# P times V of a pooled attention: four float32r products on the whole array become float32 products on parts of it

## Chip, core and metric

The kernel runs on one core of a Trainium2 chip. The metric is the device time of one execution in microseconds; the median of three runs of the kernel before is 544.26 us (543.83 to 544.35).

## What is computed

Attention over keys and values that are averaged in groups of eight tokens, and behind it a gated MLP that mixes tokens. Eight batches, eight heads, 576 tokens, head size 64; 72 pooled tokens.

```
k_p = k.reshape(B, H, 72, 8, D).mean(axis=3)
v_p = v.reshape(B, H, 72, 8, D).mean(axis=3)
scores = scale * np.matmul(q, k_p.transpose(0, 1, 3, 2))
attn = exp(scores - max); attn = attn / (sum(attn) + 1e-09)
x = np.matmul(attn, v_p)             # heads side by side: (8, 576, 512)
h = np.maximum(x @ w_in, 0.0)        # 512 -> 1024
u, v = h[..., :512], h[..., 512:]
v_n = (v - mean(v)) / np.sqrt(var(v) + 1e-06)
v_s = np.einsum('ts,bsd->btd', w_spatial, v_n) + b_spatial[None, :, None]
out = (u * v_s) @ w_out
```

All inputs are float64 or float32 in memory; the output is float32.

## The kernel before

The work is cut into steps, and each step is a generator that records its instructions up to the next `yield`. The string `ORDER` names the steps one after the other; each name there advances its step by one piece. Nothing else sorts the instructions: what stands in a queue of an engine (TensorE = PE, VectorE = DVE, ScalarE = ACT, GpSimd = POOL, and SyncE = SP, which issues all DMAs) stands there in the order of `ORDER`, and an engine that waits holds up all that is behind it in its queue.

A name starts with the batch. `K`, `KT`, `V`, `W` load and pool keys and values; `Q` loads queries; `S` computes scores of a pair of heads g (four pairs) and their softmax; `T` and `Y` turn the probabilities so that the pooled tokens lie on the partitions (`Y` for the last 64 of the 576 tokens); `A` multiplies by V. Behind them come the MLP's steps `v` (second half of h, normalised), `u` (first half), `s` (mixing of tokens, then the gate) and `o` (output). Names with `w` load weights, which come as float64 and are put together as two float32r parts, high and low, on DVE, ACT and POOL.

Large products are made of float32r products: high by high, low by high, high by low. A product whose operands are plain float32 is one call in the program and two records on PE in the trace.

A pair of heads has 2 x 72 = 144 rows of probabilities per token. 128 of them are turned into the tile `pt_h`/`pt_l` (high and low part, lines 660 and 663 for batches 2 to 7, line 194/196 for 0 and 1), the other 16, of two pairs together 32 rows, into `pt_r` and, high and low, `pt_rr` (661, 666; 689, 691). In batches 0 and 1 PE turns them (676, 680, 728, 729); in the others DVE turns blocks of 32 by 32 (698, 702) and two DMAs through DRAM finish it. On the side of V, step `W` splits the pooled values under a mask that says to which head a row belongs (`vm_h`, `vm_l`, `vr_s`, `vr`; lines 517 to 531). `att_av` (lines 767 to 770) then makes four float32r products for each pair of heads and each half of the tokens (256 and 320), in one PSUM bank of the ring `mm`, which has four; the result is split into `xT` high (ACT, line 194) and low (DVE, 196 and 775).

The scores (line 634) are float32 products of 64 rows by 64 columns of the array, four of which lie in the four quarters; they go into the ring `s` of PSUM, two buffers of two banks each.

## Time and profile before

| | |
|---|---|
| median of three runs | 544.26 us |
| span of the profiled execution, first to last instruction | 543.1 us |
| PE busy | 519.7 us (96%) |
| DVE, ACT, POOL busy | 344.5, 287.3, 285.8 us |
| first matmul starts, last one ends | 8.40 and 540.0 us |

The profiled execution's own time is its span of 543.1 us and what lies around it; the median of the runs is 1.2 us above the span. In the trace a matmul's record is longer than the step from it to the next one, because matmuls overlap; how fast PE works is read from the starts of its rows.

### The profile page before, as it was taken

What the parts mean: (1) busy time and instruction counts of PE and PEld (TensorE: products, weight loads), DVE (VectorE), ACT (ScalarE), POOL (GpSimd) and SP (SyncE); (2) the same over time, 40 slices, a digit from 0 to 9 for tenths busy, and PEclk for the clock granted to TensorE, in tenths of its full rate; (3) what the DMA queues carried; (4) which work ended last, traced back from release to release, by engine and by line L of the source; (5) the groups of instructions that cost most, each with busy time, mean ns of one, the idle gap of its engine ahead of it and who ended that gap; (6) DMA issues with size and microseconds to landing.
All of it is one profiled execution on the core that took longest, in us unless ns stands there. A gap on an engine that the chain in (4) does not pass through costs nothing.

```text
span 543.1 us, 11804 instructions
## 1 busy us (share of the span) xinstructions
PE 519.7 (96%) x4317; PEld 468.6 (86%) x4317; DVE 344.5 (63%) x787; ACT 287.3 (53%) x919; POOL 285.8 (53%) x380
## 2 busy tenths in 40 slices
PE   3669999999999999999999999999999999999997
PEld 3556898988998999999898898998998898998996
DVE  3998989999966865775755756657743645234110
ACT  2677887545845566575464465565552544134122
POOL 3536666775488747764575965155345325124141
PEclk9979999999999999999999999999999999999999
DMA  7987654456447664654357133450053113000102
GB/s 216 286 208 151 155 144 120 107 118 171 139 154 188 176 160 116 161 148 114 93 138 186 64 86 74 121 159 1 25 181 98 56 39 95 21 0 21 59 20 78
DMA packets 125674, 63.11 MB, mean 116 GB/s; under 512 B 84272, under 2 KB 109360, under 8 KB 125616
## 3 DMA queue, kind: packets, MB, share of 16 engines
q1 hardware_dynamic: 125616, 62.35, 43.0%
q8 instruction: 34, 0.56, 0.4%
q14 instruction: 24, 0.20, 0.1%
HBM read 44.92 MB, written 17.40 MB: 115 GB/s over the span
## 4 chain that ended last, share of the span: by engine, by line
PE 92%; DVE 3%; DMA 2%; ACT 1%; SPq 1%; issue 0%; ACTq 0%
PE mm L879 19%; PE mm L861 19%; PE mm L905 18%; PE mm L818 17%; PE s_ps L634 4%; PE mm L834 3%; DMA qt<-in_q 2%; PE tp L767 2%; PE tp L770 2%; PE tp L768 2%; PE mm L880 2%; PE tp L769 2%; PE mm L881 2%; PE tp L374 1%; DVE vr_s L517 1%
## 5 line engine op out<-in xcount | busy, mean ns | idle before, releaser
L861 PE MATMUL mm<-xT,win_h 128*128 128x256 f32 (+1 forms) x512 | 103.7, 296 | 0.0
L893 POOL TENSOR_TENSOR gT<-g,gT 128x256 fp32r<-128x256 f32 x64 | 47.4, 746 | 88.3 <-ACT gT L890 88.3
L861 PEld LDWEIGHTS mm<-xT,win_h 128*128 128x128 f32 x512 | 83.0, 188 | 1.7
L818 PE MATMUL mm<-win_h,xT 128*128 128x512 f32 x256 | 80.5, 395 | 0.0
L905 PE MATMUL mm<-wout_h,gT 128*128 128x512 f32 (+1 forms) x264 | 80.4, 387 | 0.0
L879 PE MATMUL mm<-wT_h,vn_h 128*128 128x320 f32 (+1 forms) x256 | 76.1, 297 | 0.1
L879 PE MATMUL mm<-wT_h,vn_l 128*128 128x320 f32 (+1 forms) x256 | 75.6, 295 | 0.0
L879 PE MATMUL mm<-wT_l,vn_h 128*128 128x320 f32 (+1 forms) x256 | 75.6, 295 | 0.0
L861 PE MATMUL mm<-xT,win_l 128*128 128x320 f32 (+1 forms) x256 | 75.5, 295 | 0.0
L884 DVE TENSOR_TENSOR g<-mm,ru 128x320 f32<-128x320 f32 (+1 forms) x64 | 28.6, 452 | 72.9 <-PE mm L881 62.1
L828 POOL TENSOR_TENSOR vn_l<-vv,vn_h 128x512 fp32r<-128x512 f32 x32 | 42.6, 1337 | 39.3 <-ACT vn_h L826 39.0
L617 POOL TENSOR_TENSOR e<-e,rs 128x576 f32<-128x576 f32 (+1 forms) x32 | 42.9, 1341 | 35.7 <-DVE rs L615 25.7
L610 ACT ACTIVATE e<-s_ps,mx 128x72 f32<-128x72 f32 x174 | 53.0, 340 | 5.9 <-DVE mx L596 5.8
L905 PEld LDWEIGHTS mm<-wout_h,gT 128*128 128x128 f32 x264 | 48.0, 188 | 8.9
L818 PEld LDWEIGHTS mm<-win_h,xT 128*128 128x128 f32 x256 | 47.0, 188 | 9.6
L905 PE MATMUL mm<-wout_l,gT 128*128 128x512 f32 (+1 forms) x132 | 50.9, 385 | 0.0
L818 PE MATMUL mm<-win_l,xT 128*128 128x512 f32 x128 | 50.6, 395 | 0.0
L864 ACT ACTIVATE ru<-mm 128x256 f32<-128x256 f32 (+1 forms) x64 | 25.4, 412 | 46.5 <-PE mm L861 39.0
L879 PEld LDWEIGHTS mm<-wT_h,vn_h 128*128 128x128 f32 x256 | 48.2, 188 | 1.4 <-ACT ob L909 0.4
L805 POOL TENSOR_TENSOR rstd<-rstd,small 128x1 f32<-128x1 f32 (+1 forms) x40 | 24.4, 616 | 46.9 <-DVE rstd L803 46.7
L879 PEld LDWEIGHTS mm<-wT_h,vn_l 128*128 128x128 f32 x256 | 48.3, 189 | 0.8
L879 PEld LDWEIGHTS mm<-wT_l,vn_h 128*128 128x128 f32 x256 | 48.3, 189 | 0.0
(193 smaller groups left out, 1227.3 us busy)
## 6 DMA issues: line engine op xcount, KB each, us to landing
st<-in_k SPq DMA_DIRECT2D x32, 256.0 KB, 4.1
qt<-in_q SPq DMA_DIRECT2D x112, 72.0 KB, 3.0
out<-ob SPq DMA_DIRECT2D x31, 256.0 KB, 2.2
st<-in_v SPq DMA_DIRECT2D x24, 256.0 KB, 3.6
xd<-X SPq DMA_DIRECT2D x24, 256.0 KB, 2.2
pt_l<-xd SPq DMA_DIRECT2D x24, 256.0 KB, 3.1
stw<-in_moe_w_in SPq DMA_DIRECT2D x8, 512.0 KB, 5.2
st<-in_v SPq DMA_DIRECT2D x4, 512.0 KB, 4.2
```

Of the source, the lines that this page charges most:

```text
L610: nc.scalar.activation(em[:, h, :], sv[:, h % 2, h // 2, :], AF.Exp, bias=mx[:, h:h + 1], scale=QK, accum_out=sm[:, h:h + 1])
L617: nc.gpsimd.tensor_tensor(em, em, rs.unsqueeze(2).broadcast_to([P, n, SP]), op=ALU.mult)
L634: nc.tensor.matmul(s_ps[i * TL:(i + 1) * TL, e, c * SP:(c + 1) * SP], lhsT=lhs, rhs=kT[es, pair, :], start=True, stop=True)
L805: nc.gpsimd.tensor_tensor(rstd[:m], rstd[:m], neg_half[:m], op=ALU.pow)
L818: nc.tensor.matmul(a, lhsT=xT[:, i, o + c * P:o + (c + 1) * P], rhs=w[:, i, DH:], start=(i == 0 and j == 0), stop=(i == NK - 1 and j == 2))
L828: nc.gpsimd.tensor_tensor(t["vn_l"][:, c, :], vv, f32(t["vn_h"][:, c, :]), op=ALU.subtract)
L861: nc.tensor.matmul(a, lhsT=w[:, i, d * P:(d + 1) * P], rhs=xT[:, i, o + ts.start:o + ts.stop], start=(i == 0 and j == 0), stop=(i == NK - ...
L864: nc.scalar.activation(t["ru"][:, d, ts], a, AF.Relu)
L879: nc.tensor.matmul(a, lhsT=x[:, c, ds], rhs=y[:, c, ts], start=(c == 0 and j == 0), stop=False)
L884: nc.vector.tensor_tensor(g, a, t["ru"][:, d, ts], op=ALU.mult)
L893: nc.gpsimd.tensor_tensor(dst[:, d, 1, at:at + m], g[:, o:o + m], f32(dst[:, d, 0, at:at + m]), op=ALU.subtract)
L905: nc.tensor.matmul(a, lhsT=src[:, i, x, at:at + m], rhs=w[:, i, cols], start=(i == 0 and j == 0), stop=(i == ND - 1 and j == 2))
```

## The change

Pairs of heads are formed two apart: pair g = 2j + i holds the heads 4j + i and 4j + i + 2. Of the 72 pooled tokens of a head, 64 now make the main tile and 8 the rest: `pt` (128 rows, two heads by 64, for each of the two pairs of a j) and `pt_r` (32 rows of rest of the four heads of a j, copied four times, to the partitions 0, 32, 64 and 96). Both are plain float32. The split of the probabilities, the split of V (`W`), their tiles and masks are gone. Pooled V is used as it is (`vp`); the rest of pooled V (`vs`, 32 rows) is summed on DVE or POOL instead of PE in batches 0 and 1, and DVE writes it four times to `vr` under a mask (`rest_values`). The softmax's last step on POOL writes the main and the rest part in calls of their own.

P times V has a step of its own, `P`, for two pairs of heads at once. It takes both buffers of the PSUM ring `s`. First come four products of 32 rows by 128 columns of the array, one for each of the four copies and each into its own bank, then for each half of the tokens four products of 64 by 64, in the quarters of the array. Step `A` (`att_x`) only splits the result into `xT`. For batches 0 and 1, PE writes the four copies of the rest as products with the identity; for the others the rest is read four times by DMA, and the main tile is written to DRAM in two DMAs instead of one. `ORDER` is another string throughout.

```diff
-    "wv3~ wv3 wv3 0K^ 0Q1^ 0K 0Q0~^ 0V^ 0Q1 wv3 0K 0K 0K 0K 0Q0 0K 0V 0Q1 0Q0 0S0 wv3 0S0 0S1 0V wv1 0K 0S1 0S0 wv3 "
...
+    "0Q1^ 0Q0~^ 0K^ 0K wo1~ wo1 0Q0 wv1 0K 0K 0K 0K 0K 0Q0 wo1 0Q1 0Q1 0S1 wo1 0S0 wv1 wv1 0S0 0S0 wv1 wv1 0K 0K wv1 "
...
-    KR = 2 * SP - P
-    RR = 2 * KR
+    PT_B = 1
     KM = P // 2
+    KE = SP - KM
+    RR = 4 * KE
...
-    half, mask, neg_half = small[:, 0:4].rearrange("p (a b) -> p a b", a=2), small[:2 * RR, 4:6], small[:, 6:7]
+    neg_half, vr_of = small[:, 6:7], small[:RR, 0:4].rearrange("p (e i) -> p e i", e=2)
...
-    PE_B = 2
+    PE_B, PE_T = 2, 2
+    nc.vector.tensor_reduce(vr_of, ident[:RR, :RR].rearrange("p (e i s) -> p e i s", e=2, i=2), axis=AX.X, op=ALU.add)
...
+        vs = pl.tile([RR, 2, D], F32, name="vs", tag="vs")
+        pool_sum(rest, vs, nc.gpsimd if "!" in alt else nc.vector)
...
-    def att_values_split(vp, vr_s, half_of):
-        for e in range(2):
-            nc.scalar.activation(vm_h[:, :, e, :], vp, AF.Copy, scale=half_of[:, e:e + 1])
-        yield
-        for r in range(2):
-            nc.scalar.activation(vr[2 * r * RR:(2 * r + 1) * RR, :, 1, :], vr_s, AF.Copy)
...
-            nc.vector.scalar_tensor_tensor(vm_l[:, :, e, :], vp, half_of[:, e:e + 1], f32(vm_h[:, :, e, :]),
-                                           op0=ALU.mult, op1=ALU.subtract)
-        yield
-        nc.vector.tensor_tensor(vr[RR:2 * RR, :, 1, :], vr_s, f32(vr[0:RR, :, 1, :]), op=ALU.subtract)
...
+    def rest_values(t, vs):
+
+        t["vr"] = ring("vr", 2, [P, 2, 2, D], F32, "vr")
+        for r in range(4):
+            nc.vector.tensor_tensor(t["vr"][r * RR:(r + 1) * RR], vs.unsqueeze(2).broadcast_to([RR, 2, 2, D]),
+                                    vr_of[:, r % 2, :].unsqueeze(1).unsqueeze(3).broadcast_to([RR, 2, 2, D]), op=ALU.mult)
...
-        nc.gpsimd.tensor_tensor(em, em, rs.unsqueeze(2).broadcast_to([P, n, SP]), op=ALU.mult)
...
-        nc.gpsimd.tensor_copy(pr[:, :NC, :, odd], em[:, 1:2 * NC:2, SP - KR:])
+        rest, m = em[:, :, KM:], 2 * NC
+
+        def scaled(dst, src, by):
+            nc.gpsimd.tensor_tensor(dst, src, by.unsqueeze(2).broadcast_to(list(src.shape)), op=ALU.mult)
+
+        scaled(pr[:, :NC, :, odd, :].rearrange("p c e s -> p (c e) s"), rest[:, :m], rs[:, :m])
+        for i in range(2 if odd else 0):
+            ts = slice(i * TL, (i + 1) * TL)
+            scaled(pr[:TL, NC, :, i, :], rest[ts, m:], rs[ts, m:])
+        pm = em.rearrange("p n s -> p (n s)")[:, :2 * n * KM]
+        scaled(pm.rearrange("p (n s) -> p n s", s=KM), em[:, :, :KM], rs)
+        t["p", g] = pm[:, :NC * P].rearrange("p (c s) -> p c s", s=P)
...
+            t["pt", j] = (ring("pt", PT_B, [P, 2, S], F32, "pt"), ring("pt_r", PT_B, [P, S], F32, "pt_r"))
...
-    def split_pt(t, j, cs, alt):
-
-        ph, pw, rw, rr = t["pt", j]
-        eng = nc.gpsimd if "!" in alt else nc.vector
-        nc.scalar.activation(ph[:, :, cs], pw[:, :, cs], AF.Copy)
-        nc.scalar.activation(rr[:2 * RR, cs], rw[:, cs], AF.Copy)
...
+                for r in range(4):
+                    nc.tensor.matmul(tr[r * RR:(r + 1) * RR, c * P:(c + 1) * P],
+                                     lhsT=t["r", j][:, c].rearrange("p e i s -> p (e i s)"), rhs=ident, start=True, stop=True)
+            pt, rt = new_pt(t, j)
+            for i, (dst, src) in enumerate(((pt[:, 0], tps[0]), (pt[:, 1], tps[1]), (rt, tr))):
+                copy = nc.vector.tensor_copy if alt and i else nc.scalar.copy
+                copy(by_token(dst[:, :NC * P]), src.rearrange("p (c q t) -> p c q t", c=NC, q=4))
...
+            for e in range(2):
+                nc.sync.dma_start(out=moved[i][:, e].rearrange("a s k f -> a s (k f)"),
+                                  in_=x[:, e].rearrange("p k f -> p (k f)"))
...
+            nc.sync.dma_start(out=pt[:, i, :NC * P].rearrange("p (a f) -> p a f", a=4),
+                              in_=moved[i].rearrange("a e s k f -> (e s k) a f"))
+            yield
+        for r in range(4):
+            nc.sync.dma_start(out=rt[r * RR:(r + 1) * RR, :NC * P].rearrange("r (a f) -> r a f", a=4),
+                              in_=moved[2].rearrange("a r f -> r a f"))
...
-    def att_av(t, half, g):
-        mh, ml, _, rr = t["pt", g // 2]
-        mh, ml = mh[:, g % 2, :], ml.bitcast(F32R)[:, g % 2, :]
...
+    def att_av(t, j):
+        pt, rt = t["pt", j]
+        vr = t["vr"].rearrange("p j i d -> p j (i d)")
+        o = t["o", j] = [ring("s", 2, [P, 2, 512], F32, "o_ps", ps) for _ in range(2)]
+        for r in range(4):
+            half, e = divmod(r, 2)
+            rs, ts = slice(r * RR, (r + 1) * RR), HALF[half]
+            nc.tensor.matmul(o[half][:, e, :ts.stop - ts.start], lhsT=vr[rs, j, :], rhs=rt[rs, ts], start=True, stop=False)
+        yield
+        for half in range(2):
+            ts = HALF[half]
+            for i in range(2):
+                for e in range(2):
+                    es = slice(e * KM, (e + 1) * KM)
+                    nc.tensor.matmul(o[half][i * D:(i + 1) * D, e, :ts.stop - ts.start], lhsT=t["vp"][es, 2 * j + i, :],
+                                     rhs=pt[es, i, ts], start=False, stop=True)
+            yield
+    def att_x(t, half, g):
+        j, e = divmod(g, 2)
...
-        o = ps_tr()[:, :n]
-        h2, l2 = (x[:, g, :, :].rearrange("p e d -> p (e d)") for x in (vm_h, vm_l))
-        nc.tensor.matmul(o, lhsT=h2, rhs=mh[:, ts], start=True, stop=False)
-        nc.tensor.matmul(o, lhsT=l2, rhs=mh[:, ts], start=False, stop=False)
-        nc.tensor.matmul(o, lhsT=h2, rhs=ml[:, ts], start=False, stop=False)
-        nc.tensor.matmul(o, lhsT=vr[:, g, :, :].rearrange("p e d -> p (e d)"), rhs=rr[:, ts],
-                         start=False, stop=True)
+        o, c = t["o", j][half][:, e, :n], g
+        yield from split(xT[:, c, lo:lo + n], xT[:, c, LO + lo:LO + lo + n], o)
...
+            st[f"P{j}"] = lambda j=j: att_av(t, j)
```

On PE the place of the second pair of `A` steps in batch 3 shows what one half of an `A` step for two pairs was before (`pt_h`, `pt_l`: probabilities high and low; `vm`, `vr`: values; `mm` the MLP's products around it):

```order
L881 MATMUL mm<-wT_l,vb 128x256
L767 MATMUL tp<-pt_h,vm_h 128x320
L768 MATMUL tp<-pt_h,vm_l 128x320
L769 MATMUL tp<-pt_l,vm_h 128x320
L770 MATMUL tp<-pt_rr,vr 128x320
L767 MATMUL tp<-pt_h,vm_h 128x256
L768 MATMUL tp<-pt_h,vm_l 128x256
L769 MATMUL tp<-pt_l,vm_h 128x256
L770 MATMUL tp<-pt_rr,vr 128x256
L905 MATMUL mm<-wout_h,gT 128x512 x2
```

In the changed kernel a `P` step (here the first of batch 2) stands between products of the MLP:

```order
L865 MATMUL mm<-wout_h,gT 128x512 x2
L865 MATMUL mm<-wout_l,gT 128x512
L717 MATMUL o_ps<-pt_r,vr 128x256 x2
L717 MATMUL o_ps<-pt_r,vr 128x320 x2
L724 MATMUL o_ps<-pt,vp 64x256 x4
L724 MATMUL o_ps<-pt,vp 64x320 x4
L821 MATMUL mm<-xT,win_h 128x320 x2
L821 MATMUL mm<-xT,win_l 128x320
```

Sixteen products of the whole array for two pairs of heads, in several places, have become twelve of parts of it in one place, with whole-array products on both sides.

At the start of the program SP issued these DMAs (`qt`: queries, `st` and `st_r`: keys and values, `stw`: weights):

```order
L210 DMA stw<-in_moe_w_in 128x1024
L368 DMA st<-in_k 128x2x256 x2
L550 DMA qt<-in_q 128x4x64 x2
L381 DMA st_r<-in_k 64x1x256 x2
L550 DMA qt<-in_q 128x4x64 x2
L553 DMA qt<-in_q 64x2x64 x2
```

and now it issues:

```order
L519 DMA qt<-in_q 128x4x64 x4
L521 DMA qt<-in_q 64x2x64 x2
L351 DMA st<-in_k 128x2x256 x2
L365 DMA st_r<-in_k 64x1x256 x2
L190 DMA st<-in_moe_w_out 128x1024
L190 DMA stw<-in_moe_w_in 128x1024
```

The queries have moved ahead of the first block of weights.

On DVE the first rows before the softmax's first maximum (`mx`) were, from the first weights on:

```order
L226 TENSOR_SCALAR x<-x 128x512
L235 SCALAR_TENSOR_TENSOR x<-stw,x 128x512
L237 TENSOR_SCALAR y<-x 128x512
L240 SCALAR_TENSOR_TENSOR y<-stw,y 128x512
L575 COPY qT<-tp 128x4x4x32
L577 COPY pt_q<-tp 128x128
L594 TENSOR_REDUCE mx<-s_ps 128x2x4
```

and are now:

```order
L543 COPY qT<-tp 128x4x4x32
L545 COPY pt_q<-tp 128x128
L206 TENSOR_SCALAR x<-x 128x512
L215 SCALAR_TENSOR_TENSOR x<-st,x 128x512
L217 TENSOR_SCALAR y<-x 128x512
L220 SCALAR_TENSOR_TENSOR y<-st,y 128x512
L206 TENSOR_SCALAR x<-x 128x512
L215 SCALAR_TENSOR_TENSOR x<-stw,x 128x512
L217 TENSOR_SCALAR y<-x 128x512
L559 TENSOR_REDUCE mx<-s_ps 128x2x4
```

Seven rows on weights, of two blocks, stand ahead of the first maximum where four of one block stood, and they stand behind the copy of the queries.

## Rows read from the trace of the kernel before


**Rows 1.** The page: the span, and the busy time of each engine (share of the span, instructions).

```profile
span 543.1 us, 11804 instructions
PE 519.7 (96%) x4317; PEld 468.6 (86%) x4317; DVE 344.5 (63%) x787; ACT 287.3 (53%) x919; POOL 285.8 (53%) x380
```

**Rows 2.** What PE's matmuls waited for, over the whole span: microseconds in total, times, longest.

```profile
PE tp L567 <- DMA qt<-in_q: 9.7, 2, 8.4
PE tp L770 <- DVE vr L531: 2.7, 1, 2.7
```

**Rows 3.** Stretches of the span, in us from its start: length, then busy time and instructions of PE, PEld (its weight loads), DVE, ACT and POOL, then the granted clock, the DMA share and GB/s.

```profile
8.40:46.00 37.60, 26.48 (x377) 21.00 (x379) 29.58 (x57) 25.38 (x85) 19.34 (x21) 0.91 0.90 244
14.95:85.70 70.75, 59.71 (x679) 49.31 (x670) 63.88 (x140) 57.41 (x192) 41.33 (x45) 0.95 0.74 185
46.00:92.20 46.20, 45.59 (x506) 39.34 (x505) 41.59 (x100) 37.77 (x124) 28.63 (x32) 1.00 0.54 128
92.20:540.00 447.80, 447.66 (x3439) 408.24 (x3437) 269.50 (x618) 221.23 (x707) 235.40 (x319) 1.00 0.38 103
```

**Rows 4.** PE in order of time, around `A` steps: start and length in us, line, operation, form, count. First two pairs of heads with 320 tokens up to the MLP's next product, then one pair with 256 tokens and the start of the next.

```profile
169.03 0.32 PE L767 MATMUL tp<-pt_h,vm_h 128*128 128x320 f32 x1
...
170.22 0.64 PE L818 MATMUL mm<-win_h,xT 128*128 128x512 f32 x2
...
52.58 0.28 PE L767 MATMUL tp<-pt_h,vm_h 128*128 128x256 f32 x1
...
53.05 0.31 PE L767 MATMUL tp<-pt_h,vm_h 128*128 128x320 f32 x1
```

**Rows 5.** PE in order of time around scores (L634, quarters of the array; the count is of records, two for each product), and around L414, 8 products of 256 columns in the two column halves of the array.

```profile
90.22 0.73 PE L634 MATMUL s_ps<-kT,qT 64*64 64x72 f32 x32
90.88 0.39 PE L767 MATMUL tp<-pt_h,vm_h 128*128 128x256 f32 x1
91.11 0.27 PE L768 MATMUL tp<-pt_h,vm_l 128*128 128x256 f32 x1
...
299.74 0.30 PE L881 MATMUL mm<-wT_l,vb 128*128 128x320 f32 x1
299.97 1.23 PE L634 MATMUL s_ps<-kT,qT 64*64 64x72 f32 x64
301.02 0.30 PE L634 MATMUL s_ps<-kT,pt_q 64*64 64x72 f32 x8
301.26 0.38 PE L879 MATMUL mm<-wT_h,vn_h 128*128 128x256 f32 x1
...
45.85 1.95 PE L414 MATMUL mm<-st,pairs 128*64 128x256 f32 x16
47.63 1.10 PE L374 MATMUL tp<-pairs,st 128*64 128x64 f32 x32
```

**Rows 6.** PE in order of time: the transposes of the probabilities' rest (L680), and the pooling of the values' rest (L340), each up to the scores behind it.

```profile
23.51 0.60 PE L680 MATMUL tp<-ident,pt_p 128*32 128x128 f32 x4
24.04 0.73 PE L634 MATMUL s_ps<-kT,qT 64*64 64x72 f32 x32
...
48.66 1.14 PE L340 MATMUL mm<-st_r,ident 64*64 64x64 f32 x16
49.77 0.73 PE L634 MATMUL s_ps<-kT,qT 64*64 64x72 f32 x32
```

**Rows 7.** Instructions of DVE from the first maximum to the last normalisation of batch 0 (14.95 to 85.7 us), grouped by line and form: count, busy us, mean ns of one, idle before.

```profile
L196 DVE TENSOR_TENSOR pt_l<-tp,pt_h 128x512 fp32r<-128x512 f32 x6 | 4.0, 680 | 0.7 <-ACT pt_h L194 0.6
...
L517 DVE TENSOR_TENSOR vr_s<-vq,small 32x128 f32<-32x128 f32 x4 | 3.5, 884 | 0.0
...
L691 DVE TENSOR_TENSOR pt_rr<-tp,pt_rr 32x512 fp32r<-32x512 f32 x3 | 2.0, 682 | 0.8 <-ACT pt_rr L689 0.7
...
L528 DVE SCALAR_TENSOR_TENSOR vm_l<-vp,small,vm_h 128x256 fp32r<-128x256 f32 x4 | 1.7, 476 | 0.0
...
L735 DVE TENSOR_TENSOR pt_l<-tp,pt_h 128x128 fp32r<-128x128 f32 x3 | 0.8, 283 | 0.0
L531 DVE TENSOR_TENSOR vr<-vr_s,vr 32x256 fp32r<-32x256 f32 x2 | 0.8, 415 | 0.1
...
L740 DVE TENSOR_TENSOR pt_rr<-tp,pt_rr 32x64 fp32r<-32x64 f32 x2 | 0.4, 216 | 0.5 <-ACT pt_rr L738 0.5
```

**Rows 8.** DVE in order of time at the first maximum and at the last normalisation of batch 0; PE at the first `s` product; the mean of the two copies of the normalised values on ACT and POOL.

```profile
14.95 1.57 DVE L594 TENSOR_REDUCE mx<-s_ps 128x8 f32<-128x576 f32 x2 [0.74 <-PE s_ps L634]
...
85.12 0.54 DVE L807 TENSOR_SCALAR vv<-vv,mv,rstd 64x512 f32<-64x512 f32 x1
...
92.06 0.28 PE L879 MATMUL mm<-wT_h,vn_h 128*128 128x256 f32 x1
...
L826 ACT ACTIVATE vn_h<-vv 128x512 fp32r<-128x512 f32 x32 | 20.1, 632 | 3.0 <-DVE vv L807 2.7 <-PE mm L879 0.3
...
L828 POOL TENSOR_TENSOR vn_l<-vv,vn_h 128x512 fp32r<-128x512 f32 x32 | 42.6, 1337 | 39.3 <-ACT vn_h L826 39.0
```

**Rows 9.** SP's first DMA issues in order of time, and ACT's first work on a block of weights that has landed.

```profile
0.72 0.39 SPq L210 DMA_DIRECT2D stw<-in_moe_w_in  x1
...
2.15 1.02 SPq L550 DMA_DIRECT2D qt<-in_q  x2
...
5.51 0.66 ACT L221 ACTIVATE x<-stw 128x512 f32<-128x512 f32 x1 [3.51 <-DMA stw<-in_moe_w_in]
```

More of the change, by code (lines that the diff above doesn't have):

```diff
@@ L324, in pool_sum @@
             x, y = (t.unsqueeze(2).broadcast_to(dst.shape) for t in (x, y))
+        if dst.shape[0] < st.shape[0]:
+            for j in range(2):
+                js = slice(j * RR, (j + 1) * RR)
+                eng.tensor_tensor(dst[:, j, :], x[js, 0], y[js, 0], op=ALU.add)
+            return
         eng.tensor_tensor(dst, x, y, op=ALU.add)
@@ L427, in att_keys @@
             return
-        keys = k[b].rearrange("(r a e) (s j) d -> r e s a (j d)", r=2, e=2, j=POOL)
+        keys = k[b].rearrange("(r e a) (s j) d -> r e s a (j d)", r=2, e=2, j=POOL)
         kp = pl.tile([P, 2, 2, D], F32, name="kp", tag="kp")
@@ L437, in att_keys @@
             yield
-        st = load_rest(k[b, :, KM * POOL:, :].rearrange("h (s j) d -> h s (j d)", j=POOL))
+        st = load_rest(k[b])
         yield
@@ new lines, in att_values @@
+        if b < PE_B:
+            yield from first_values(t, b, vp, alt)
+            return
+        rows = v[b, :, :KM * POOL, :].rearrange("h (k s j) d -> h s k (j d)", k=2, j=POOL)
+        sts, g2 = [], [slice(2 * r, 2 * r + 2) for r in range(2)]
+        for r in range(2):
+            sts.append(ring("kv", 3, [P, 2, POOL * D], F32, "st"))
+            for i in range(2):
+                for e in range(2):
+                    nc.sync.dma_start(out=sts[r][e * KM:(e + 1) * KM, i, :], in_=rows[NG * r + 2 * e + i])
+            yield
@@ new lines, in att_values @@
+        st = load_rest(v[b])
+        yield
+        pe = "^" in alt or "%" in alt
+        yield from pool_half((*sts, st)[:2 if rest_engine(alt, True) else 3], alt)
+        for r in range(2):
+            if pe:
+                acc = acc if r else ps_pool()
+                pool_pe(sts[r], acc[:, g2[r], :], alt)
+            else:
+                pool_sum(sts[r], vp[:, g2[r], :], eng)
+            yield
+        vs = pl.tile([RR, 2, D], F32, name="vs", tag="vs")
+        pool_sum(st, vs, rest_engine(alt, pe) or nc.vector)
@@ L727, in att_pt_l @@
+        if b < PE_T:
             tp = ps_tr()
-            nc.tensor.transpose(out=tp[:, :P], in_=em[:, :P], identity=ident)
-            nc.tensor.transpose(out=tp[:RR, P:2 * P], in_=t["r", j][:, NC, :, :], identity=ident)
+            nc.tensor.transpose(out=tp[:, :P], in_=em, identity=ident)
+            for r in range(4):
+                nc.tensor.matmul(tp[r * RR:(r + 1) * RR, P:P + TL], lhsT=pr, rhs=ident[:TL, :TL], start=True, stop=True)
             yield
-            ph, pw, rw, rr = new_pt(t, j)
@@ L746, in att_pt_l @@
         yield
-        m = ring("xdl", 2, [2, 2, P, 32], F32, "xdl", dr)
-        nc.sync.dma_start(out=m.rearrange("i a (s k) t -> (i a s) (k t)", k=4), in_=x.rearrange("p k t -> p (k t)"))
+        m = ring("xdl", 2, [2, 2, 2, 32, 2, 32], F32, "xdl", dr)
+        for e in range(2):
+            nc.sync.dma_start(out=m[:, :, e].rearrange("i a s k t -> (i a) s (k t)"),
+                              in_=x[:, e].rearrange("p k t -> p (k t)"))
         mr = ring("xdlr", 2, [2, RR, 32], F32, "xdlr", dr)
```

198 lines of the change are left out of this document (57 added, 141 removed), and 128 rows, old and new, of the table ORDER.

## The prediction

> **What bounds the kernel now.** I read the page first: PE is busy for 519.7 of 543.1 us [rows 1], so PE sets the time wherever it is packed. The stretches of the span tell where that is [rows 3]. From 92.2 to 540.0 us PE is busy for 447.66 of 447.80 us at the full granted clock (1.00, its level of 2.4 GHz), and from 46 to 92.2 for 45.59 of 46.20. From 8.4 to 46 it is busy for only 26.48 of 37.60. So there are three parts. Up to the first matmul at 8.40 us PE waits for the queries: 8.4 is the longest wait of the list of waits [rows 2]. Up to 46 us it lacks 11.1 us, the largest single wait being 2.7 for `vr` from DVE. Then PE is the path to the end. DVE is the engine nearest to it early on: from its first maximum at 14.95 to the last normalisation of batch 0, at 85.12, it is busy for 63.88 of 70.75 us [rows 3, 8]. A saving on PE behind 92 us shortens the span one for one; ahead of that point it does so only if DVE allows it. The mark between the two is the first `s` product at 92.06 [rows 8], which needs the normalised values of all of batch 0.
>
> **P times V.** An `A` step of two pairs of heads with 320 tokens takes 170.22 - 169.03 = 1.19 us for eight products, .149 each; one pair with 256 tokens takes 53.05 - 52.58 = .47 for four, .118 each [rows 4]. Two pairs and both halves: 8 x .149 + 8 x .118 = 2.14 us, which happens 16 times.
>
> The trace has fp32 products on parts of the array in two places. The 8 products of L414, two at a time in column halves, take 47.63 - 45.85 = 1.78 us [rows 5]: 16 records in 8 shared passes of 256 columns, .22 each, so a product needs two passes and 320 columns cost .275 a pass. Scores show that four quarters share as well: 32 records take 90.88 - 90.22 = .66 us, 64 and the 8 behind them 301.26 - 299.97 = 1.29. That is ten more passes of four for .63 us, .063 each for 72 columns, which agrees with .22 for 256. The quarter products of `P` then take 2 x .22 + 2 x .275 = .99 us. The four products of the rest, in four strips of 32 rows, take two shared passes of 320, .55, if the strips share as quarters do. Together 1.54 us.
>
> Changing from whole array to parts and back is not free. At the scores of 90.22, the eight passes make .50 of the .66 us, so .16 goes in them; the first product behind takes 91.11 - 90.88 = .23 instead of .118, .11 more; and 299.74 + .149 = 299.89 against a start of 299.97 is .08 on the way in [rows 5]. One excursion costs .35 us. `P` changes three times (whole, strips, quarters, whole). No row shows the middle change. It costs nothing more at best, and a whole excursion at worst, so .35 to .70; I take .50, since it lacks the return to the whole array. The Trainium skill ("TensorEngine Tiling (Array Packing)", Key Properties) says that changing the tiling mode drains the array. That speaks against the change, and the trace agrees with its .35 us; it gives no price, so the sum stays on the rows. So `P` takes 1.54 + .50 = 2.04 us, saves .10, and 16 of them save 1.6 us (bounds: 4.0 saved, 1.6 lost). Thirteen stand behind the first `s` product: 1.3 us.
>
> **Other PE work.** In batches 0 and 1, four `T` steps make the rest's copies with 16 products of 128 columns in column quarters: 8 passes of .11 (half of .22), .88, and about .35 for the change, 1.23 us, where the four transposes of L680 took 24.04 - 23.51 = .53 [rows 5, 6]: +.70, and four times +2.8. The rest of V is no longer pooled on PE (L340): 49.77 - 48.66 = 1.11 us a batch, 2.2 for two [rows 6]. Keys, scores, weights and the MLP have the same products. Ahead of the first `s` product: +2.8 - 2.2 - .3 (three `P`s), and by the order about 2.0 us of batch 1's turning and scores come ahead of it that stood behind: +2.3. Behind it: -1.3 - 2.0 = -3.3.
>
> **The start.** SP issued the first block of weights at .72 and its data were in use by 5.51; the queries were issued at 2.15, and PE started at 8.40 [rows 2, 9]. Now the queries are issued first. Landing like that first block, they give a start between 5.5 and 6.5; I take 6.0, a gain of 2.4 us. What it is worth depends on DVE: seven rows on weights of two blocks now stand ahead of the first maximum, four of one block before. With the second block behind queries and keys, I expect that maximum at about 15 as before, against 14.95.
>
> From there to the last normalisation DVE loses 4.0 + 3.5 + 2.0 + 1.7 + .8 + .8 + .4 = 13.2 us (split of probabilities and of V [rows 7]). It gains eight writes of `vr`, by L531's .415, 3.4 us, and the sums of the rest, eight small ones: by the rows for 32 to 128 partitions, 4 x .216 + 2 x .415 + 2 x .283 = 2.3. No row shows an operation under this mask; the bounds are .28 (L735) and .88 (L517) for a write, -1 and +3.7 us. And 10.7 us of work is now ahead of that point in its order which stood behind (another block of queries, of keys, more of batch 1's softmax and `xT`). 63.88 - 13.2 + 5.7 + 10.7 = 67.1, +3.2 us. At the old idle time the last normalisation starts at 85.12 + 3.2 = 88.3, and with its own .54, the copies on ACT (.63) and POOL (1.34) [rows 8] the first `s` product could start at 90.8. By PE it is 92.06 - 2.4 + 2.3 = 92.0 with the old waits; the wait for `vr`, 2.7, may shrink since that write needs no split now. I take 91.5, between the two routes.
>
> ACT and POOL lose the halves of the same splits and POOL takes more calls for the softmax's last step; neither is near PE (287.3 and 285.8 us busy [rows 1]). SP issues about a hundred DMAs more, at .4 to .5 us each [rows 9] some 45 us of a queue of 543; the probabilities of batches 2 to 7 are turned a batch ahead, some 56 us (447.8 us over eight batches [rows 3]), and this covers it. Uncovered, `P` waits; that is in a rival below.
>
> **The sum.** Behind 92.06 the profiled execution took 543.1 - 92.06 = 451.0 us. 91.5 + 451.0 - 3.3 = 539.2 us of span. The median of the runs is 1.2 us above the span: 540.4.
>
> **The rivals.** *The start gains nothing* (chance .12): the second block lands late, the first maximum comes 3.5 us later, and the first `s` product is at 95. Span 542.7, 543.9 in the runs: the same. For it speaks that DMA is already busy at .90 from 8.4 to 46 [rows 3].
>
> *P and scores wait for each other* (.13), the one on the other side. `P` takes both buffers of ring `s`, which scores alone used before, so it waits until DVE and ACT have read the scores (about .78 us for a maximum [rows 8]), and the next scores wait for the splits of `xT` (at most .68 each, by the row of the same line with 512 columns [rows 7]). The order keeps some 6 us of PE work between scores and `P` and 10 between `P` and scores, so a wait needs a queue of DVE or ACT, or a late DMA of probabilities, that is 5 us behind. The gain of 3.9 us is spent at 3.9 / 16 = .24 us a `P`; at .5 us more than that is gone: 540.4 + 8 = 548.4, slower.
>
> *The strips don't share* (.10). No row shows a product of 32 rows. Two at a time they take .44 + .55 = .99 instead of .55: +.44 x 16 = 7, 547.4; one at a time 2 x .44 + 2 x .55 = 1.98: +1.43 x 16 = 23, 563. It turns the sign from .55 + .24 = .8 us on. The Trainium skill ("TensorE: Matmul & The Clock Gate", Measured speedup vs the span model) gives 3.07 times for four strips of 32 rows with 512 columns, hence an estimate of 1.98 / 3.07 = .65 us instead of .55, and 540.4 + 1.6 = 542.0; no row shows it, and the sum does not use it.
>
> *More is gained* (.05): batch 0's waits of 11.1 us shrink with the shorter chain from V to `P`, and the middle change is free: 535 or less.
>
> **How the numbers follow.** The forecast (.60) has its own range, 536 to 543.1: `P`'s bounds are -2.4 and +3.2, the masked write's -1 and +3.7. A measurement of this kernel can tell .2% from no change, so 543.2 and 545.3 part the signs. Faster: .60 + .05 = .65. Same: .12. Slower: .13 + .10 = .23. The range must leave out no more than 2 in 10: it goes from 533.5 to 549, takes in the first rival, that of the waits, and strips that share in pairs, and leaves out strips that don't share at all and the waits' long end.
>
> **What would show it.** In the trace after, `P` should go from its first strip to the product behind it in 2.0 to 2.1 us, strips .55 and quarters .99; starts of two strips a pass apart would show that they don't share. The first matmul should start near 6, the first maximum near 15, the first `s` product near 91.5. From there to the last matmul PE should have no idle time, 445 us; waits of `o_ps` or `s_ps` on ACT or DVE would be the second rival. The forecast is wrong if `P` takes over 2.3 us, or if the first `s` product comes after 95.

## The result and the profile after

The changed kernel takes 551.7 us (median of four runs, 550.5 to 554.3) against 544.3 for the kernel before in the same comparison: ratio 1.0137, 95% interval 1.0111 to 1.0163. It is 1.4% slower, where 0.7% faster was forecast. The profiled execution took 551.63 us. The kernel before, measured again beside each experiment below, took 544.7 to 545.0 us there.

The page of the changed kernel, span and busy time of each engine (before: [rows 1]):

```profile
span 549.8 us, 12189 instructions
PE 526.7 (96%) x4553; PEld 451.4 (82%) x4553; DVE 312.9 (57%) x720; ACT 246.2 (45%) x813; POOL 280.8 (51%) x391
```

PE is busy 7.0 us longer and the span is 6.7 us longer, while VectorE (DVE) and ScalarE (ACT) lost 32 and 41 us. It is tempting to stop here and say that PE's stream grew. The experiments below speak against that as the whole cause. What PE waited for in the changed kernel (before: [rows 2]):

```profile
PE tp L535 <- DMA qt<-in_q: 5.0, 1, 5.0
PE tp L632 <- POOL e L606: 2.7, 2, 2.1
...
PE o_ps L717 <- DVE vr L502: 0.5, 1, 0.5
```

The marks of the path, from PE in order of time: the strips for the second half of the tokens in the first `P`, which wait for the last write of `vr`; the pooling of batch 1's values; the first `s` product (before: 92.06, [rows 8]):

```profile
35.23 1.88 PE L717 MATMUL o_ps<-pt_r,vr 32*128 32x320 f32 x4 [0.49 <-DVE vr L502]
...
50.68 0.65 PE L401 MATMUL mm<-st,pairs 128*64 128x256 f32 x4
...
99.07 0.38 PE L839 MATMUL mm<-wT_h,vn_h 128*128 128x256 f32 x1
```

and from DVE: the first weight row, the first maximum, the last normalisation of batch 0 (before: 14.95 and 85.12, [rows 8]):

```profile
12.84 0.43 DVE L206 TENSOR_SCALAR x<-x 128x512 uint32<-128x512 uint32 x1 [5.80 <-ACT x L201]
...
16.80 0.75 DVE L559 TENSOR_REDUCE mx<-s_ps 128x8 f32<-128x576 f32 x1
...
96.07 0.50 DVE L767 TENSOR_SCALAR vv<-vv,mv,rstd 128x512 f32<-128x512 f32 x1
```

With these marks the start falls into stretches. For the kernel before they are: first maximum to the first product with `vr`; pooling of batch 1's values to the first `s` product (columns as in [rows 3]):

```profile
14.95:33.30 18.35, 10.78 (x205) 8.09 (x195) 17.66 (x30) 13.77 (x42) 8.30 (x10) 1.00 0.89 259
45.85:92.06 46.21, 45.60 (x504) 39.34 (x505) 41.62 (x99) 37.91 (x124) 28.78 (x32) 1.00 0.54 128
```

and for the changed kernel: first maximum to those strips of the first `P`; from there to the pooling of batch 1's values; from there to the first `s` product; then the whole from first maximum to last normalisation, and all behind the first `s` product:

```profile
16.88:35.20 18.32, 13.74 (x189) 9.22 (x185) 17.53 (x30) 14.55 (x56) 13.63 (x17) 0.91 0.88 248
35.20:50.68 15.48, 13.72 (x221) 9.48 (x222) 12.15 (x28) 9.68 (x43) 9.15 (x8) 0.78 0.93 211
50.68:99.07 48.39, 44.45 (x514) 35.47 (x513) 45.20 (x99) 30.42 (x92) 30.32 (x32) 1.00 0.64 146
...
16.80:96.60 79.80, 69.62 (x828) 52.30 (x828) 73.04 (x150) 53.02 (x183) 50.83 (x55) 0.94 0.75 184
99.06:546.40 447.34, 445.95 (x3503) 389.74 (x3496) 232.18 (x551) 185.98 (x615) 225.88 (x328) 1.00 0.40 103
```

The reader should see this sum. First maximum: 16.80 against 14.95, +1.85. From it to the first product that needs the last write of `vr`: 18.4 us here (35.23; the first strips ran at 33.69 on copies already written) against 18.3 before (33.28), although the splits, 13 us of DVE rows over the whole start, were gone. On to the pooling of batch 1's values: 15.5 against 45.85 - 33.28 = 12.6, +2.9. On to the first `s` product: 48.4 against 46.2, +2.2. Together 99.07 - 92.06 = 7.0 us. Behind that point 447.3 us to the last matmul against 447.9, a gain of .6 where 3.3 were forecast.

In the third stretch PE is busy 44.45 of 48.39 us and DVE 45.20, where before PE was busy 45.60 of 46.21 and DVE 41.62. The chain that ends last also changed engines there: from 45.8 to 92 us it lay on PE before, but for some 3 us on ACT at 79 to 82, now it runs mostly along DVE from 16.9 to 35.2 us, from 55 to 69 and from 84 to 96.

Why DVE takes as long with less to do is seen where it meets GpSimd (POOL). DVE in order of time, rows on a weight block whose usual lengths are .42, .69, .42 and .69 us:

```profile
25.11 0.41 DVE L206 TENSOR_SCALAR x<-x 128x512 uint32<-128x512 uint32 x1
25.55 1.63 DVE L215 SCALAR_TENSOR_TENSOR x<-stw,x 128x512 uint32<-128x512 uint32 x1
27.29 1.30 DVE L217 TENSOR_SCALAR y<-x 128x512 uint32<-128x512 uint32 x1
28.63 1.65 DVE L220 SCALAR_TENSOR_TENSOR z<-stw,y 128x512 fp32r<-128x512 uint32 x1
```

and POOL over the same time:

```profile
25.24 1.39 POOL L606 TENSOR_TENSOR e<-e,rs 128x640 f32<-128x640 f32 x1
26.60 1.71 POOL L238 TENSOR_TENSOR x<-x,wout_h 128x512 f32<-128x512 f32 x1
28.39 1.34 POOL L240 TENSOR_TENSOR wout_l<-x,y 128x512 fp32r<-128x512 f32 x1
```

The first row (25.11) runs for .41 and meets POOL only in its last .28 us. Each of the next three begins while a POOL row is under way and ends .28 to .55 us after that POOL row's end (26.63, 28.31, 29.73), as if it had stood still until then. I call the excess over the shortest row of the same form a collision, where it is over .15 us. Summed over the rows from the first maximum to the last normalisation, collisions are 12.3 us in the changed kernel (16 rows) and 5.3 in the kernel before (6 rows). The Trainium skill ("SBUF — State Buffer", SBUF: two separate sides) says that GpSimd and certain kinds of DVE instruction share a pair of ports as an exclusive lock, held for a whole instruction, so that the other one blocks. These rows agree with it, and the prediction did not use it.

The arithmetic of `P` itself came out as forecast. PE around the first `P` of batch 2, with the MLP's products on both sides:

```profile
155.09 0.40 PE L865 MATMUL mm<-wout_l,gT 128*128 128x512 f32 x1
155.41 0.82 PE L717 MATMUL o_ps<-pt_r,vr 32*128 32x256 f32 x8
156.16 1.20 PE L724 MATMUL o_ps<-pt,vp 64*64 64x256 f32 x16
157.29 0.56 PE L821 MATMUL mm<-xT,win_h 128*128 128x320 f32 x2
157.69 0.31 PE L821 MATMUL mm<-xT,win_l 128*128 128x320 f32 x1
```

The step from the first strip to the product behind the quarters is 1.88 us (155.41 to 157.29). The product ahead, 512 columns at .231, should have ended its step at 155.32, so .09 goes on the way in; two products of 320 columns take .40 instead of .29 behind it, .11. That is 2.08 us against 2.14 before and 2.04 forecast. Strips and change take .75, quarters and the way out 1.13.

### The profile page after: what moved, and what is told of

Read it like the earlier page. It is cut to its first block, busy times and chain, and to the rows that moved or that the text cites. A ratio compares the mean times of both kernels' runs of the same rounds, so it can differ in the third digit from the quotient of the medians.

```text
span 549.8 us, 12189 instructions
## 1 busy us (share of the span) xinstructions
PE 526.7 (96%) x4553; PEld 451.4 (82%) x4553; DVE 312.9 (57%) x720; ACT 246.2 (45%) x813; POOL 280.8 (51%) x391
## 3 DMA queue, kind: packets, MB, share of 16 engines
q1 hardware_dynamic: 135568, 64.12, 45.8%
## 4 chain that ended last, share of the span: by engine, by line
PE 79%; DVE 10%; DMA 3%; POOL 2%; ACT 2%; issue 2%; SPq 1%; DVEq 0%; POOLq 0%; ACTq 0%
PE mm L839 18%; PE mm L821 16%; PE mm L865 16%; PE mm L778 13%; PE s_ps L597 3%; PE o_ps L724 3%; PE mm L794 3%; PE o_ps L717 2%; PE mm L840 1%; PE mm L841 1%; DVE x L215 1%; DMA st<-in_moe_w_out 1%; DVE mx L559 1%; DVE vv L767 1%; DMA out<-ob 1%
## 5 line engine op out<-in xcount | busy, mean ns | idle before, releaser
L839 PE MATMUL mm<-wT_h,vn_h 128*128 128x256 f32 (+1 forms) x256 | 76.6, 299 | 0.6 <-ACT ob L869 0.6
L839 PE MATMUL mm<-wT_h,vn_l 128*128 128x256 f32 (+1 forms) x256 | 75.7, 296 | 0.0
L839 PE MATMUL mm<-wT_l,vn_h 128*128 128x256 f32 (+1 forms) x256 | 75.7, 296 | 0.0
L844 DVE TENSOR_TENSOR g<-mm,ru 128x256 f32<-128x256 f32 (+1 forms) x64 | 28.2, 451 | 67.9 <-PE mm L841 55.0
L865 PEld LDWEIGHTS mm<-wout_h,gT 128*128 128x128 f32 x264 | 48.1, 188 | 10.7 <-issue 1.0
L850 ACT ACTIVATE gT<-g 128x256 fp32r<-128x256 f32 x64 | 26.0, 415 | 67.1 <-DVE g L844 63.5
L176 DVE TENSOR_TENSOR xT<-o_ps,xT 128x256 fp32r<-128x256 f32 (+1 forms) x64 | 28.2, 450 | 40.3 <-ACT xT L174 40.2
L839 PEld LDWEIGHTS mm<-wT_l,vn_h 128*128 128x128 f32 x256 | 48.4, 189 | 0.0
```

Of the source, the lines that this page charges most:

```text
L176: nc.vector.tensor_tensor(lo, src, f32(hi), op=ALU.subtract)
L839: nc.tensor.matmul(a, lhsT=x[:, c, ds], rhs=y[:, c, ts], start=(c == 0 and j == 0), stop=False)
L844: nc.vector.tensor_tensor(g, a, t["ru"][:, d, ts], op=ALU.mult)
L850: nc.scalar.activation(dst[:, d, 0, at:at + m], g[:, o:o + m], AF.Copy)
L865: nc.tensor.matmul(a, lhsT=src[:, i, x, at:at + m], rhs=w[:, i, cols], start=(i == 0 and j == 0), stop=(i == ND - 1 and j == 2))
```

## The experiments

Two theories went into the first runs. **Theory D**: DVE's rows set the first `s` product. **Theory P**: PE's own stream sets it, which is 7.0 us longer, much of it because PE works at half rate for longer: in the changed kernel from 5.0 to about 18 us and from 28.8 to 42.5. All runs below are edits of the changed kernel, but for the one marked; their times compare with its 551.7 (550.5 to 554.3), whose runs spread by 3.8 us, so that a difference of 1 us is not told from none. The marks, the busy times and the collisions come from one profiled execution of each kernel.

**Copies of pooled V on ACT.**

```diff
+            if b < PE_B:
+                for i in range(2):
+                    nc.scalar.activation(t["vr"][r * RR:(r + 1) * RR, :, i, :], vs, AF.Copy, scale=vr_of[:, r % 2, i:i + 1])
+                continue
```

> The 16 writes of the copies under the mask in batches 0 and 1 (8 on VectorE, 4.0 us) become 16 small ones on ScalarE. Theory D (from the first maximum to the first `s` product VectorE is the bound: 73.0 of 79.8 us busy): the first `s` product comes 3 to 4 us earlier than 99.1, and the time falls from 551.7 to about 548. Theory P (TensorE's own path bounds the start: its half clock and the longer `T` steps): the time changes by under 1 us.

552.4 us. From the first maximum to the last normalisation DVE is busy 3.5 us less, and yet the stretch is as long:

```profile
17.60:96.80 79.20, 67.92 (x824) 50.69 (x824) 69.59 (x142) 58.19 (x199) 50.59 (x55) 0.94 0.78 185
```

PE now waits for ACT, which has eight small rows in one place of its queue:

```profile
PE mm L233 <- ACT win_h L228: 2.9, 1, 2.9
```

The work was handed on along with the wait for it. Theory D fails in its simple form; theory P forecast a change under 1 us, which came, but with a new wait for ACT beside it, so it is not confirmed.

**Weights first.**

```diff
-    "0Q1^ 0Q0~^ 0K^ 0K wo1~ wo1 0Q0 ...
+    "wo1~ 0Q1^ 0Q0~^ 0K^ 0K wo1 0Q0 ...
```

> One part of the change undone: the DMA of the first weight block is issued ahead of the queries again. Theory D: VectorE's weight rows, which waited for that block until 12.84 us, run while the queries land, the first maximum comes at 15 instead of 16.8, and the time falls by 1.5 to 2 us although TensorE starts some 3 us later. Theory P: TensorE starts at about 8.4 instead of 5.0, and the time rises by 1 to 3 us.

552.3 us. PE started at 6.90 and the first maximum came at 17.5, since the seven rows ahead of it belong to two blocks and the second landed late (its rows began at 15.96 us). No gain and no loss beyond the spread: neither the gain of 1.5 to 2 us nor the loss of 1 to 3 us that the theories forecast.

**`wo1` later.** The six entries of `wo1` move from the start of `ORDER` to a place ahead of `wo0`; its DVE rows run from 107.5 us on.

> The second weight block of the output (`wo1`), not used before 190 us, is loaded and split behind the first `s` products instead of at the start. VectorE loses four rows (2.3 us) ahead of the first `s` product and GpSimd three rows of about 1.3 us, which VectorE's rows collide with. Theory D: the first `s` product 3 to 5 us earlier, the time about 548. Theory P: under 1 us.

556.5 us. The first `s` product did come 3.7 us earlier, as theory D has it:

```profile
95.33 0.39 PE L839 MATMUL mm<-wT_h,vn_h 128*128 128x256 f32 x1
```

But the stretch behind it took 453.6 instead of 447.3 us, and PE waited there for the rows by which DVE frees the buffers of ring `s`:

```profile
95.33:548.90 453.57, 448.12 (x3502) 391.28 (x3496) 234.31 (x555) 186.81 (x617) 228.94 (x330) 0.99 0.40 103
```

```profile
PE s_ps L597 <- DVE xT L735: 3.0, 1, 3.0
```

DVE is 82 to 97% busy from 100 to 150 us in the changed kernel. What is taken out of the start and put there is paid there.

**TensorE kept warm.** Six steps of four identity products (`wd0` to `wd5`) stand between 20 and 30 us.

> 24 products of the identity with itself are added on TensorE between 20 and 30 us, where it waits, to see what its half clock from 28.8 to 42.5 us costs. If they keep the clock up, TensorE's chain from 35.2 to 43.8 us (strips, quarters, key pooling) shrinks by about 4 us. Theory P: the time falls by 3 to 4 us. Theory D: VectorE, next on the chain from 52.7 us on, takes up part of it: 0 to 2 us.

554.0 us (552.7 to 555.2). The clock did stay up. The stretch 28.8 to 42.5 us of the changed kernel, with 5.0 to 18 ahead of it, and then this run's:

```profile
5.00:18.00 13.00, 10.00 (x161) 8.60 (x161) 5.76 (x11) 4.08 (x9) 0.88 (x1) 1.00 0.82 221
28.80:42.50 13.70, 13.08 (x131) 8.25 (x133) 12.57 (x25) 7.64 (x20) 7.09 (x9) 0.63 0.83 185
```

```profile
28.80:42.50 13.70, 11.10 (x169) 7.96 (x169) 13.05 (x27) 9.58 (x29) 6.67 (x9) 1.00 0.80 189
```

Key pooling, 80 records from 39.16 to 43.13 us in the changed kernel, took 2.5 us here instead of 4.0 (from 38.05):

```profile
38.05 1.15 PE L358 MATMUL tp<-pairs,st 128*64 128x64 f32 x32
```

It ended 2.6 us earlier. PE then waited 1.4 us for a row of `xT` on DVE, so that the next scores came 1.1 us earlier, and 1.7 us for DVE's `pt_q`. Then the half rate came back where the changed kernel ran at 1.00:

```profile
46.00:48.00 2.00, 2.00 (x60) 1.79 (x56) 0.79 (x1) 1.00 (x8) 1.85 (x3) 0.50 1.10 297
```

From the scores at 45.67 (46.77 in the changed kernel) to the pooling of batch 1's values at 50.80 (50.68) PE took 5.13 us instead of 3.91, and the rest of the gain was gone. The first `s` product came .5 us earlier, at 98.53, and the time did not fall. So the half rate of 28.8 to 42.5 us is not worth the 3 to 4 us of theory P, since DVE takes up the better part of it; how much the other 1.2 us would have given, had the clock stayed up, this run does not show.

**Key pooling of batch 2 on POOL.** `2K~` becomes `2K!` in `ORDER`.

> The pooling of batch 2's keys (six rows, 5.0 us as they ran) goes from VectorE to GpSimd, which is busy for 50.8 of the 79.8 us from the first maximum to the first `s` product. Theory D (VectorE's work sets the time up to some 150 us, where it is 82 to 97% busy): 3 to 5 us faster than the changed kernel, about 548. Theory P (TensorE's own stream sets it): within 1 us. A third outcome, as when the copies went to ScalarE: the work is paid again on the engine that takes it, no gain although VectorE is freer.

554.4 us, and the first `s` product 3.1 us later, at 102.20. DVE lost six rows and was busy for longer:

```profile
16.80:99.20 82.40, 68.65 (x817) 51.20 (x815) 74.72 (x144) 53.25 (x183) 57.18 (x61) 0.94 0.72 177
```

74.72 against 73.04 us: collisions rose from 12.3 to 15.3. DVE and POOL are no two separate places for work of this kind.

**Softmax unscaled in batches 0 and 1.**

```diff
+        if b < 2:
+            nc.gpsimd.tensor_copy(pm.rearrange("p (n s) -> p n s", s=KM)[:, :1], em[:, :1, :KM])
+        else:
+            scaled(pm.rearrange("p (n s) -> p n s", s=KM), em[:, :, :KM], rs)
```

> GpSimd leaves out the main part of the softmax's last step in batches 0 and 1 (the probabilities stay unscaled), 8 rows of some 1.2 us. Of the 12.3 us by which VectorE's rows ran longer than the shortest of their form in the changed kernel, 4.4 lay beside these rows. Theory D: VectorE's rows lose 3 to 4 us, the first `s` product comes 3 to 5 us earlier than 99.1, and the time is about 547 to 549. Theory P: within 1 us.

547.4 us, 4.3 faster. No DVE row was touched, and DVE's busy time fell by 6.1 us, as collisions fell from 12.3 to 6.3 us:

```profile
16.60:91.40 74.80, 67.00 (x819) 51.75 (x816) 66.93 (x150) 52.84 (x183) 43.56 (x55) 0.98 0.80 196
```

```profile
94.44 0.39 PE L842 MATMUL mm<-wT_h,vn_h 128*128 128x256 f32 x1
```

The first `s` product came 4.6 us earlier and the stretch behind it was the same (447.0). POOL's results also reached PE earlier (waits for `e`, 2.7 us above, fell to .7), so this run shows what POOL's eight rows cost, not how it divides between the two.

**Without `wo1`.** Its entries are gone from `ORDER`, and the output's products take block 0 for it.

> The output's weight block `wo1` is left out (its products use block 0 instead, so the number of products is the same): the work that came back behind the first `s` product when it was only put later is gone now. Theory D: the first `s` product at about 95.3 as there, and the gain stays: 547 to 548. Theory P: within 1 us.

549.3 us; first `s` product at 97.08, 2.0 earlier, 447.1 behind it. With nothing added later the gain stays, smaller than expected (547 to 548 us, first `s` product at about 95).

**Warm from the start.** `wd0` to `wd5` stand at the start and in the first waits.

> 24 products of the identity with itself stand at the start of TensorE's queue and in its first waits. If they bring the clock up before the queries land, the work from 5.0 to 18 us, done at half rate before, shrinks by up to 5 us. Theory P: 2 to 4 us faster. Theory D: the first maximum stands behind seven weight rows on VectorE that end at 16.8 us whatever TensorE does: within 1 us.

555.1 us (551.2 to 558.9), first `s` product at 98.44. Key pooling ran at full rate here; 32 records span 1.15 us, where 32 spanned 1.97 in the changed kernel:

```profile
8.26 1.15 PE L358 MATMUL tp<-pairs,st 128*64 128x64 f32 x32
```

```profile
16.27 1.97 PE L358 MATMUL tp<-pairs,st 128*64 128x64 f32 x32
```

No gain in the time, and .6 us in the first `s` product. The first maximum still came at 16.91, behind DVE's seven rows. But here, too, the half rate moved: from 20 to 28 us the granted clock was .57, where the changed kernel had 1.00. The two stretches were not kept at full rate together in any run.

**Low parts on PE.** `wo1~` and `wv3~` become `wo1~^` and `wv3~^`, with a second buffer for `z`.

> The low parts of two weight blocks of the start (`wo1`, `wv3`) are formed on TensorE (three products each, 1.8 us at full clock, where it waits anyway) and ScalarE instead of by two GpSimd rows of 1.3 us each. Theory D with collisions (a VectorE row beside a GpSimd row runs until that one ends): VectorE's rows before the last normalisation lose 1 to 3 of the 12.3 us, the first `s` product comes 1 to 2 us earlier, and the time falls by 1 to 2 us to about 550. Theory P: TensorE has 3 to 4 us more, half of it in waits: 1 to 2 us slower.

551.7 us, first `s` product at 98.87. Collisions fell to 8.7 us, by 3.5 where 1 to 3 were expected, but nothing was gained. PE came to the pooling of batch 1's values earlier and waited there for them to land:

```profile
PE mm L401 <- DMA st<-in_v: 1.4, 1, 1.4
```

The pooling came at 49.32, 1.4 us earlier. From it to the first `s` product PE had 45.9 us of work instead of 44.5, and the stretch took 49.6 us instead of 48.4. So fewer collisions alone do not shorten the start.

**No strips in batches 2 to 7.**

```diff
+            if b < 2:
                 nc.tensor.matmul(o[half][:, e, :ts.stop - ts.start], lhsT=vr[rs, j, :], rhs=rt[rs, ts], start=True, stop=False)
...
-                                     rhs=pt[es, i, ts], start=False, stop=True)
+                                     rhs=pt[es, i, ts], start=b >= 2, stop=True)
```

> The four strips of 32 rows are left out of `P` in batches 2 to 7 (the rest of the pooled tokens is not added), 12 of 16 steps. By the rows of the changed kernel a `P` step is 2.08 us, of which .75 from the first strip to the first quarter. If `P` is paid in full where TensorE is packed, the time falls by 12 x .75 = 9 us, to about 542.7, and the stretch behind the first `s` product by as much; if strips and changes of the array's use are hidden beside the products around them, by clearly less.

545.3 us (544.4 to 546.8): -6.4, where 9 were expected. PE's busy time behind the first `s` product fell from 445.95 to 437.38, 8.6 us, .71 a `P`:

```profile
99.10:540.00 440.90, 437.38 (x3406) 385.35 (x3400) 230.00 (x551) 185.39 (x615) 225.85 (x328) 1.00 0.41 105
```

So the work of a `P` is paid in full where PE is packed; 2 us came back as waits (PE idle there 3.5 us instead of 1.4, the most of it for ACT's and DVE's rows at 162 and 220 us).

**Scaling of batch 0 on ACT.**

```diff
+        if b < 1:
+            for h in range(2 * n):
+                nc.scalar.activation(pm[:, h * KM:(h + 1) * KM], em[:, h, :KM], AF.Copy, scale=rs[:, h:h + 1])
+        else:
...
```

> In batch 0 the main part of the softmax's last step goes from GpSimd (four rows of some 1.2 us) to ScalarE (36 small rows, some .25 us each). Theory D with collisions: VectorE loses 1.5 to 2.5 us of collisions and the first `s` product comes 1 to 2 us earlier, unless ScalarE, with 9 us more, takes the chain over as it did with the copies of pooled V: then no gain or 1 to 3 us slower. Theory P: within 1 us.

558.0 us. Collisions fell to 7.4 us and DVE to 68.5, but the stretch grew to 86 us, with PE waiting for ACT:

```profile
17.00:103.10 86.10, 70.80 (x824) 51.73 (x824) 68.53 (x150) 64.83 (x219) 45.40 (x51) 0.88 0.69 170
```

```profile
PE tp L636 <- ACT e L615: 5.2, 8, 1.6
```

**The kernel before, with DVE's split of probabilities done twice in batches 0 and 1** (the same instruction a second time).

> The kernel before, with VectorE's split of the turned probabilities in batches 0 and 1 (eight rows of .68 us, six of them ahead of the first `s` product, 4.1 us) done twice. Theory D (VectorE sets the first `s` product in either order): the kernel before slows by 3 to 5 us, to about 548, and its first `s` product comes 3 to 4 us later than 92.06. Theory P (there TensorE sets it: its chain ran on TensorE from 45.8 us on): under 1.5 us.

547.8 us against 544.8, ratio 1.0051 (1.0033 to 1.0069): 3.0 us for 4.1 us of added rows ahead of the first `s` product (six of eight), which moved from 92.06 to 94.65.

So the start of the kernel before, too, has little room on DVE, although its chain ran on PE from 45.8 us.

**DVE alone relieved, POOL alone relieved**, with nothing handed on. In the first, `pool_sum` of batch 2's keys becomes one sum; in the second `nc.gpsimd.tensor_tensor(as_w(x), as_w(x), f32(hi), op=ALU.subtract)` is left out for three blocks.

> VectorE leaves out four of the six rows that pool batch 2's keys (the halving steps; a sum of two tokens stands for the mean of eight), 4.0 us as they ran, at 62 to 65 and 93 us; nothing goes to another engine. Theory D: the first `s` product 3 to 4 us earlier than 99.1 and the time at 548 to 549. If the chain is mainly one of landings (values of batch 1 land at about 51 us in most of these runs), the rows lie behind that landing and the gain is the same; if TensorE sets it, under 1 us.

> GpSimd leaves out one of its two rows for the low part of three weight blocks of the start (`wo1`, `wv1`, `wv3`), some 1.3 to 1.7 us each; nothing goes to another engine. Theory D with collisions: VectorE's rows lose 1.5 to 2.5 us and the first `s` product comes 1 to 2 us earlier. If the landing of batch 1's values at about 51 us is the next limit, as where these parts went to TensorE: no gain ahead of that landing, under .7 us in all.

551.3 and 550.5 us; first `s` products at 97.8 in both, 1.3 and 1.2 us earlier; DVE from first maximum to last normalisation:

```profile
17.20:95.30 78.10, 67.00 (x817) 51.07 (x817) 71.09 (x146) 52.88 (x183) 50.10 (x55) 0.95 0.78 188
```

```profile
16.70:94.90 78.20, 67.00 (x830) 50.47 (x832) 71.64 (x150) 53.26 (x184) 46.85 (x52) 0.98 0.77 187
```

POOL's rows gave what was expected of them at the first `s` product; in the times, -.4 and -1.2 us are no more than the spread. DVE's edit took out less than its expectation says: the six rows at 62 to 65 us took 3.6 us in the changed kernel, and the two that stand for them take .6, so 3.1 us went and not 4.0 (the rows at 93 stayed). DVE's busy time fell by only 1.95, because another row, that of the bias (`wT_l<-bt`), now started while a POOL row was under way (67.31 to 68.63 us) and took 1.78 us, to 69.24, instead of .76. So the 1.3 us are two thirds of what DVE was really relieved of; PE is nearly packed beside it (44.45 of 48.39 us above). As far as these runs show, no one engine is the bound of the whole start: DVE is the one up to the first `P`, where it was busy for 17.53 of 18.32 us, and behind it DVE, POOL, landings and PE each stand within a us or two of the bound.

## Why the prediction was wrong

**The step that failed** is the route by DVE: "63.88 - 13.2 + 5.7 + 10.7 = 67.1 ... At the old idle time the last normalisation starts at 85.12 + 3.2 = 88.3". It started at 96.07. Two terms make up the 7.8 us. The first maximum came at 16.80, not 15: the block of weights that stands ahead of it reached DVE at 12.84, behind the queries, after 5.8 idle us; the four rows of that block and the three of the next end at 16.8. And the rows took 73.0 us, not 67.1; the idle time was as forecast. I had priced each row by its mean in the old order, and that mean holds the collisions of that order. Of the 3.5 us that I took off for four rows of `vr_s`, 2.4 were one collision (the other three rows take .27 to .31 us):

```profile
23.50 2.67 DVE vr_s L517
```

Moving rows changes which of them stand beside a POOL row, and collisions rose by 7.0 us, from 5.3 to 12.3. Of the 18.4 us from the first maximum to the strips at 35.23, 5.5 are collisions; of the 18.3 before, 3.9. The run without POOL's scaling, which changes no DVE row, takes 6.1 us off DVE and 4.3 off the time. PE itself started at 5.03, earlier than the 6.0 forecast; that gained nothing.

**What followed from the late first `P`.** The loads of batch 1's values were issued in SP's queue at (before, then after):

```profile
32.51 5.05 SPq L407 DMA_DIRECT2D st<-in_v  x2
```

```profile
41.18 0.90 SPq L393 DMA_DIRECT2D st<-in_v  x2
...
43.25 0.88 SPq L393 DMA_DIRECT2D st<-in_v  x2
```

The first of them 8.7 us later, the last 6.5 (43.66 against 37.18, each within these rows). The later ones waited for the pooling of batch 1's keys on PE, as they did before (1.9 us there), and that pooling now stands behind the first `P`, at 39.16 instead of 35.17:

```profile
SPq L393 <- PE tp L358: 0.8, 2, 0.6
```

The prediction counted SP's issues, not what they wait for. The values' pooling on PE came 6.5 us behind the last of the main ones (43.25 to 44.13); where PE was ready earlier (warm start, low parts on PE, POOL relieved), it waited .9 to 1.4 us for them to land. In the changed kernel itself it did not wait there, so the landing is the next limit and not the one that set 50.68; ahead of it PE had waited 1.7 us for DVE's `pt_q` and run at half rate. What of the 2.9 us of this stretch is due to which is not shown. In most runs the first `s` product came 47 to 50 us after that pooling (45.8 without POOL's scaling, 51.0 with the keys on POOL), so a delay there mostly goes on.

**The route by PE** failed as well, by 8.9 us of work ahead of the first `s` product against 2.3 forecast: half rate for longer (by an estimate from PE's busy time at half rate some 4.8 us more than before, at 5 to 18 and 28.8 to 42.5 us), and the rest's copies in the steps `Y`, forgotten (2.1 us where .9 stood). The copies in `T` came to the forecast 4.9 us for four, but by luck: three took 1.01 us where 1.23 stood, and the first, at half rate, 1.85. Taking the half rate away in one stretch or the other gained .5 and .6 us at the first `s` product and nothing in the time, with some of it back in a later stretch each time; so this error is not shown to set the time, and what it would give in both stretches together is open.

**P times V** was right: 2.08 us against 2.04, strips share the array (their starts lie 6 to 7 ns apart in the trace), changes cost .20 around it. The size of the term was never more than 1.6 us. The gain was .06 a step. One of the 13 steps behind the first `s` product took 2.73 us instead of 1.88, and in that one the strips did not start together but over 1.2 us. Its copies of the rest were issued by SP just ahead of it:

```profile
236.38 1.88 SPq L706 DMA_DIRECT2D pt_r<-xdlr  x4
```

```profile
238.65 1.67 PE L717 MATMUL o_ps<-pt_r,vr 32*128 32x256 f32 x8
```

The last of the four was issued .8 us before the step, in the other eleven steps of batches 2 to 7 2.9 us or more. That fits a wait for their landing, which the prediction took as covered; no wait is recorded in this trace, but the run without POOL's three rows records one of .15 us at that step, for that DMA.

**Behind the first `s` product** 3.3 us were forecast and .6 came: -1.9 of work moved ahead (2.0 forecast), about 0 for `P` instead of -1.3 (the late step is .85 of it), and +1.2 of waits, one for the split that frees ring `s` (.8 us, ending at 163.8) and one of .6 us for ACT, ending at 222.1. The rival of ring `s` is there, but small: .8 us in all, where the sign needed 3.9.

**The rivals.** "The start gains nothing" put the first `s` product at 95 for a late second block of weights and a first maximum 3.5 us later. Something near it came, and smaller: DVE waited for the first of the two blocks, and the maximum came 1.85 us later. With the collisions beside it the first `s` product went past 95 to 99.07. The strips' rival did not come, but for the one late step. The range ended at 549.

**Open.** Which part of the 7.0 us belongs to the new steps and which to the new order is not separated: the old order with the new steps was not tried. How the loss from POOL divides between blocked DVE rows and late results for PE is not separated either. That the collisions lengthen DVE's rows is shown by rows that were not touched; that they alone set the 7.0 us is not: with 3.5 us of them gone (low parts on PE) the first `s` product came only .2 us earlier. No variant here beats the kernel before.
